# A gated attention-and-MLP kernel: Wv loaded in chunks, the first x tiles turned one by one, two small loads moved to GpSimd

## Chip, cores, metric

The kernel runs on one core of a Trainium2 chip. The metric is the device time of one launch in microseconds (us). A profile also gives the *span*, from the first to the last instruction that it counts.

## The reference, cut to what matters

```python
g = sigmoid((x * gate_w).sum(-1, keepdims=True))        # x: 2048 x 448, bf16
qkv = x @ wqkv                                           # 16 heads of 28
pq, pk = q @ w_phi, k @ w_phi                            # per head
phi_q, phi_k = [softmax(p), softmax(-p)]                 # joined
a = (phi_q @ (phi_k.T @ v)) / (phi_q @ sum(phi_k) + 1e-6) @ wo
b = gelu(x @ w1 + b1) @ w2 + b2
return g * a + (1 - g) * b
```

The kernel multiplies Wq and Wk by w_phi first (the products are called Wpq and Wpk) and carries gate_w as a 449th column of Wv, so that the gate comes out of the value matmuls.

## The kernel before

The opening, cut to the parts that the change touches. `SP`, `ACT` and `POOL` below are the engines behind `nc.sync`, `nc.scalar` and `nc.gpsimd`.

```python
for m, eng in ((0, nc.scalar), (1, nc.sync)):            # first 512 rows of x, in two halves
    eng.dma_start(x0[:, 2*m:2*m+2, :], x[m*256:(m+1)*256, :].rearrange("(t p) d -> p t d", p=P))
nc.scalar.dma_start(WvG[:, 0:3, 0:D], ...)               # Wv, 336 KB
nc.scalar.dma_start(WvG[64:P, 3, 0:D], ...)              # Wv, last 64 rows
nc.sync.dma_start(gate[0:1, :], gate_w[None, :])
nc.scalar.dma_start(wphi[:, 0:3, :], ...)
load_wT(WkT, D); load_wT(WqT, 0); load_x(1)              # transposing loads, all on SP
nc.scalar.dma_start(wphi[0:64, 3, :], wphi_rows[384:448, :])
...
dummies(7)                       # warm TensorE up
turn_x0(0, xp[0])                # 8 TensorE transposes, one copy by VectorE
turn_gate()                      # gate column -> WvG, by ScalarE
turn_x0(1, xp[1])                # 8 more, one copy by ScalarE
fill_bd()                        # VectorE, from wphi
v_pair(0, on_act=True); v_pair(1)
prep(WkT, ...); prep(WqT, ...)   # Wpk, Wpq
nc.sync.dma_start(b1c[0:NJ, :], B_b1...)
load_x(2); swap_w(WqS, Wpq); swap_x(0)    # SP: WqS and xS hold the halves of Wpq and xT swapped
load_x(3); swap_w(WkS, Wpk); swap_x(1)    # to the other 64 partitions, so that
swap_w(WvS, WvG)                          # two 64-row matmuls can run side by side
... # w1, wo loads on SP
# TensorE: k_pair, v_pair; then q pairs (need WqS, xS); k_two (WkS, xS); v_two (WvS); MLP; output
```

The softmax here doesn't subtract the row's maximum and nothing guards it: scores larger than these inputs give would overflow.

Of the kernel before, what the change touches and what calls it, by code (L numbers as in the profile page):

```python
# [13 lines left out]
D = 448  # L14
# [3 lines left out]
P = 128  # L18
# [4 lines left out]
NC4 = 4  # L23
NJ = 14
# [4 lines left out]
HP = 64  # L29

BF16 = mybir.dt.bfloat16
# [4 lines left out]
def kernel(  # L36
# [14 lines left out]
    nc = tc.nc  # L51
    x = A_x[0]
# [6 lines left out]
    ps = psx.enter_context(tc.tile_pool(name="ps", bufs=3, space=PSUM))  # L59
# [7 lines left out]
    turn = [0]  # L67

    def four(name):
        turn[0] += 1  # L70
        return wide(name) if turn[0] % 4 == 0 else pair(name)


    xT = consts.tile([P, NC4, S], BF16, name="xT")
# [11 lines left out]
    ident = consts.tile([P, P], BF16, name="ident")  # L86
# [11 lines left out]
    WvG = attn.tile([P, NC4, D + 1], BF16, name="WvG")  # L98
# [5 lines left out]
    WkT = attn.tile([P, NG, D], BF16, name="WkT")  # L104
    WqT = attn.tile([P, NG, D], BF16, name="WqT")
    wphi = attn.tile([P, NC4, DH], BF16, name="wphi")
# [4 lines left out]
    b1c = w2_sb[:, 6, 0:P]  # L111
    nc.gpsimd.memset(b1c, 0.0)
    warm = w2_sb[:, 0, 0:P]
    gate = w2_sb[:, 1, :]
# [3 lines left out]
    nc.vector.memset(WvG[0:64, 3, :], 0.0)  # L118
    nc.vector.memset(wo_sb[64:P, 3, :], 0.0)
    nc.vector.memset(Wpk[0:64, 3, :], 0.0)  # L120
    nc.vector.memset(WkT[0:1, 0, 0:1], 0.0)
    wphi_rows = A_w_phi.rearrange("h a b -> (h a) b")
    x0 = oT[:, 0, 0:4 * D].rearrange("p (t d) -> p t d", t=4)
    for m, eng in ((0, nc.scalar), (1, nc.sync)):
        eng.dma_start(x0[:, 2 * m:2 * m + 2, :],
                      x[m * 256:(m + 1) * 256, :].rearrange("(t p) d -> p t d", p=P))
    nc.scalar.dma_start(WvG[:, 0:3, 0:D],
                        A_wqkv[0:384, 2 * D:3 * D].rearrange("(c p) n -> p c n", p=P))
    nc.scalar.dma_start(WvG[64:P, 3, 0:D], A_wqkv[384:448, 2 * D:3 * D])
    nc.sync.dma_start(gate[0:1, :], gate_w[None, :])  # L130
    nc.scalar.dma_start(wphi[:, 0:3, :], wphi_rows[0:384, :].rearrange("(c p) b -> p c b", p=P))

    def load_x(b):
# [7 lines left out]
    def swap_x(h):  # L141
# [5 lines left out]
    load_wT(WkT, D)  # L147
    load_wT(WqT, 0)
    load_x(1)
    nc.scalar.dma_start(wphi[0:64, 3, :], wphi_rows[384:448, :])  # L150


    first = consts.tile([1, 1], F32, name="first")
# [1 line left out]
    nc.gpsimd.memset(ident[:], 1.0)  # L155
    nc.gpsimd.affine_select(out=ident[:], in_=ident[:], pattern=[[-1, P]],
                            compare_op=ALU.is_equal, fill=0.0, base=0, channel_multiplier=1)
    nc.gpsimd.memset(hmask[:], 1.0)
    nc.gpsimd.affine_select(out=hmask[:], in_=hmask[:], pattern=[[P, NC4], [-DH, H]],
                            compare_op=ALU.is_ge, fill=0.0, base=0, channel_multiplier=1)  # L160
# [31 lines left out]
    def copy(on_act, out, in_):  # L192
        if on_act:
            nc.scalar.copy(out=out, in_=in_)
        else:
            nc.vector.tensor_copy(out=out, in_=in_)  # L196
# [3 lines left out]
             v_ps[:, :, 0:D].rearrange("p i (x d) -> p i x d", x=NPR))  # L200
        copy(on_act, lg[:, tiles], v_ps[:, :, D])

    def v_pair(u, on_act=False, b1=False):
        v_ps = four("v_ps")
        for i in range(2):
            t = 2 * u + i
            for c in range(NC4):
                nc.tensor.matmul(v_ps[:, i, 0:D + 1], lhsT=xT[:, c, t * P:(t + 1) * P],  # L208
                                 rhs=WvG[:, c, :], start=(c == 0), stop=(c == NC4 - 1))
        if b1:  # L210
            nc.tensor.matmul(v_ps[:, 1, 480:480 + NJ], lhsT=b1c, rhs=ident[:, 0:NJ],
                             start=True, stop=True, skip_group_check=True)
        v_out(u, v_ps, slice(2 * u, 2 * u + 2), on_act)
        if b1:
            nc.vector.tensor_copy(out=b1T[:], in_=v_ps[:, 1, 480:480 + NJ])
# [114 lines left out]
                    in0=src[rows, :, i, :],  # L330
                    in1=mask[rows, None, :].to_broadcast([PW, NG, PW + 2]), op=ALU.mult)

    def turn_x0(m, tp):
        for i in range(2):
            for c in range(NC4):
                lo = c * P if c < 3 else 320
                nc.tensor.transpose(tp[:, c, i * P:(i + 1) * P], x0[:, 2 * m + i, lo:lo + P],
                                    ident[:])
        copy(m == 1, xT[:, :, m * 256:(m + 1) * 256], tp[:])

    def turn_gate():
        g_ps = four("g_ps")
        for c in range(NC4):
            lo = c * P if c < 3 else 320
            nc.tensor.matmul(g_ps[:, 0, c:c + 1], lhsT=gate[:, lo:lo + P], rhs=ident[:, 0:1],
                             start=True, stop=True)
        nc.scalar.copy(out=WvG[:, 0:3, D], in_=g_ps[:, 0, 0:3])  # L347
        nc.scalar.copy(out=WvG[HP:P, 3, D:D + 1], in_=g_ps[HP:P, 0, 3:4])

    def dummies(n):  # L350
        w_ps = four("warm_ps")
        for _ in range(n):
            nc.tensor.matmul(w_ps[:, 0, :], lhsT=warm, rhs=warm[:, None, :].to_broadcast([P, 4, P]),
                             start=True, stop=True)


    dummies(7)
    xp = [ps.tile([P, NC4, 256], BF16, name="xp", tag="pair", bufs=3) for _ in range(2)]
    turn[0] += 2
    turn_x0(0, xp[0])  # L360
    turn_gate()
    turn_x0(1, xp[1])
    fill_bd()
    v_pair(0, on_act=True)
    v_pair(1)
    prep(WkT, wk_at, (1, 0, 1))
    prep(WqT, wq_at, (1, 0, 0))
    def swap_w(W_S, W):
        nc.sync.dma_start(W_S[0:HP, :, :], W[HP:P, :, :])  # L369
        nc.sync.dma_start(W_S[HP:P, 0:3, :], W[0:HP, 0:3, :])  # L370

    nc.sync.dma_start(b1c[0:NJ, :], B_b1.rearrange("(j p) -> j p", p=P))
    load_x(2)
    swap_w(WqS, Wpq)
    swap_x(0)
# [170 lines left out]
```

## Time and profile before

| | before |
|---|---|
| time, median of three runs | 156.25 us |
| span of the profiled run | 154.9 us |
| time of the profiled run | 156.61 us |
| TensorE busy | 149.4 us |

The page has a line of the busy share of the 16 DMA engines in 40 slices of the span, and one of the bytes:

```profile
DMA  5999999999995000000000001114332123334401
...
HBM read 6.11 MB, written 1.84 MB: 51 GB/s over the span
```

The engines of the DMA are busy in the first 48 us, nearly idle for some 40 us after that and at most half busy to the end, so this is a kernel whose opening is fed by transfers and whose rest is fed by TensorE. The views that the prediction reads are the chain (what ended last, followed back from the end) and the timeline (instructions in order of time: start, duration, engine, line, operation, and in brackets the idle time before it and what ended it). SPq is the queue of transfers that SP issues.

### The profile page before, as it was taken

The numbers are of one execution on the slowest core, as the hardware profiler recorded it, in microseconds if no ns is written. First come the engines' busy times: TensorE is split into PE (matmuls) and PEld (weight loads), VectorE is DVE, ScalarE is ACT, GpSimd is POOL, SyncE is SP. The second block draws the span as 40 slices with busy tenths as digits, with TensorE's granted clock in tenths as the row PEclk, the third lists the DMA queues.
The fourth block names the chain that finished last, engine by engine and source line by source line (L and its number), as shares of the span: only waits on it lengthen the run. The fifth ranks groups of instructions, "written<-read, shape, count | busy, mean of one in ns | idle before, by whom it ended". The sixth has DMA issues, their size and how long they took to land.

```text
span 154.9 us, 3180 instructions
## 1 busy us (share of the span) xinstructions
PE 149.4 (96%) x1302; PEld 83.8 (54%) x1302; DVE 83.2 (54%) x246; ACT 77.1 (50%) x90; POOL 31.8 (21%) x34
## 2 busy tenths in 40 slices
PE   7799999999999999999999999999999999999991
PEld 2475545566666864444444455555556555555581
DVE  3444999288892050000000049999977999977100
ACT  0659759998889626777767650111311111111121
POOL 7900489919776000000000000000000000000000
PEclk9999999999999999999999999999999999999999
DMA  5999999999995000000000001114332123334401
GB/s 147 255 199 146 190 235 248 221 221 212 213 336 176 4 0 4 0 0 4 0 0 0 4 0 34 34 38 96 86 101 64 40 64 90 81 85 37 122 31 30
DMA packets 28270, 14.91 MB, mean 96 GB/s; under 512 B 20062, under 2 KB 27872, under 8 KB 28256
## 3 DMA queue, kind: packets, MB, share of 16 engines
q1 hardware_dynamic: 27024, 14.06, 42.0%
q10 hardware_dynamic: 1232, 0.66, 1.5%
q8 instruction: 10, 0.16, 0.5%
q14 instruction: 4, 0.03, 0.1%
HBM read 6.11 MB, written 1.84 MB: 51 GB/s over the span
## 4 chain that ended last, share of the span: by engine, by line
PE 79%; SPq 13%; DMA 3%; issue 1%; DVE 1%; ACT 0%; ACTq 0%
PE y L485 27%; PE hp L426 27%; PE y L491 8%; PE nm L441 4%; PE pq L307 4%; PE v_ps L291 4%; SPq L135 3%; SPq L139 3%; SPq L136 3%; DMA WvS<-WvG 3%; PE pk L299 3%; PE acc L318 2%; SPq L369 1%; SPq L370 1%; SPq L144 1%
## 5 line engine op out<-in xcount | busy, mean ns | idle before, releaser
L485 PE MATMUL y<-w_sb,gel 128*128 128x448 bf16 (+1 forms) x238 | 45.2, 341 | 0.0
L426 PE MATMUL hp<-xT,w_sb 64*128 64x512 bf16 x196 | 42.6, 376 | 0.0
L426 PE MATMUL hp<-xS,w_sb 64*128 64x512 bf16 x196 | 42.3, 376 | 0.0
L431 ACT ACTIVATE gel<-hp,b1T 128x1024 bf16<-128x1024 f32 x28 | 30.8, 1111 | 13.0 <-PE hp L426 13.0
L494 ACT ACTIVATE res<-y,ungate 128x448 bf16<-128x448 f32 (+1 forms) x17 | 10.4, 612 | 50.4 <-PE y L491 50.2
L485 PEld LDWEIGHTS <-gel 128*128 128x128 bf16 x238 | 23.1, 98 | 19.0
L426 PEld LDWEIGHTS <-w_sb 64*128 64x128 bf16 x392 | 20.5, 94 | 21.6
L268 POOL TENSOR_TENSOR phik<-phik,rec 128x1792 bf16<-128x1792 bf16 (+1 forms) x8 | 25.0, 3129 | 16.1 <-DVE rec L265 16.1
L446 DVE COPY st<-nm 128x32 f32<-128x32 f32 x32 | 4.5, 184 | 35.5 <-PE nm L441 35.5
L462 DVE TENSOR_TENSOR tmp<-nm,al 128x448 bf16<-128x448 f32 x32 | 18.4, 617 | 0.0
L263 DVE TENSOR_REDUCE sums<-phik 128x64 f32<-128x1792 bf16 x8 | 16.0, 2006 | 2.6 <-ACT phik L256 2.6
L491 PE MATMUL y<-wo_sb,oT 128*128 128x448 bf16 (+1 forms) x68 | 14.7, 341 | 0.0
L307 PE MATMUL pq<-xT,Wpq 64*128 64x512 bf16 x56 | 13.2, 376 | 0.0
L307 PE MATMUL pq<-xS,WqS 64*128 64x512 bf16 x56 | 11.5, 376 | 0.1
L196 DVE CAST vaug<-v_ps 128x896 bf16<-128x896 f32 x7 | 7.5, 1074 | 6.0 <-PE v_ps L291 3.6
L312 ACT ACTIVATE EqP<-pq 128x1024 bf16<-128x1024 f32 x8 | 8.3, 1041 | 3.7 <-PE pq L307 3.7
L313 ACT ACTIVATE EqN<-pq 128x1024 bf16<-128x1024 f32 x8 | 8.3, 1042 | 0.0
L441 PE MATMUL nm<-KVbd,EqP 128*128 128x120 bf16 x64 | 8.3, 216 | 0.0
L441 PE MATMUL nm<-KVbd,EqN 128*128 128x120 bf16 x64 | 8.3, 216 | 0.0
L255 ACT ACTIVATE phik<-pk 128x896 bf16<-128x896 f32 x8 | 7.5, 940 | 1.4 <-PE pk L277 1.4
L491 PEld LDWEIGHTS <-oT 128*128 128x128 bf16 x68 | 6.1, 98 | 3.3
L208 PE MATMUL v_ps<-WvG,xT 128*128 128x449 bf16 x32 | 6.6, 354 | 1.0 <-ACT WvG L347 1.0
(90 smaller groups left out, 145.7 us busy)
## 6 DMA issues: line engine op xcount, KB each, us to landing
w_sb<-in_B_w_dram SPq DMA_DIRECT2D x4, 784.0 KB, 14.2
out_dram<-res SPq DMA_DIRECT2D x15, 112.0 KB, 1.9
w_sb<-in_B_w_dram SPq DMA_DIRECT2D x1, 1568.0 KB, 17.3
xS<-xT SPq DMA_DIRECT2D x2, 256.0 KB, 4.0
xS<-xT SPq DMA_DIRECT2D x2, 192.0 KB, 4.3
WvG<-in_A_wqkv_dram ACTq DMA_DIRECT2D x1, 336.0 KB, 4.5
wo_sb<-in_A_wo_dram SPq DMA_DIRECT2D x1, 336.0 KB, 17.0
WqS<-Wpq SPq DMA_DIRECT2D x1, 256.0 KB, 4.6
```

Of the source, the lines that this page charges most:

```text
L263: nc.vector.reduce_sum(out=sums[:], in_=ph, axis=AX.X)
L268: eng.tensor_tensor(out=ph[:, lo:hi], in0=ph[:, lo:hi], in1=rec[:, lo:hi, :, None].to_broadcast([P, hi - lo, 2, DH]), op=ALU.mult)
L307: nc.tensor.matmul(pq[:, i, :], lhsT=w_half(Wpq, WqS, i, k)[:, g * P:(g + 1) * P], rhs=x_half(i, k, h), start=(k == 0), stop=(k == NK - 1))
L312: nc.scalar.activation(out=EqP[:, g, dst], in_=src, func=ACT.Exp)
L313: nc.scalar.activation(out=EqN[:, g, dst], in_=src, func=ACT.Exp, scale=-1.0)
L426: nc.tensor.matmul(hp[:, i, :], lhsT=w1_sb[i * HP:(i + 1) * HP, k, j * P:(j + 1) * P], rhs=x_half(i, k, h), start=(k == 0), stop=(k == NK ...
L431: nc.scalar.activation(out=gel[h][:, j, :], in_=hp[:].rearrange("p a b -> p (a b)"), func=ACT.Gelu_apprx_tanh, bias=b1T[:, j:j + 1])
L441: nc.tensor.matmul(nm[s][:, g * 2 * KW:(g + 1) * 2 * KW], lhsT=E[:, g, tok], rhs=KVbd[:, g, s, :], start=True, stop=True)
L462: nc.vector.tensor_tensor(out=tmp[:, s, :].rearrange("p (x h d) -> p x h d", x=NPR, h=2), in0=nmv[s][:, :, 0:PW].rearrange("p x (h d) -> p ...
L485: nc.tensor.matmul(y, lhsT=gel[t // 8][:, j, (t % 8) * P:(t % 8 + 1) * P], rhs=w2_sb[:, j, cols], start=(j == 0), stop=False)
L491: nc.tensor.matmul(y, lhsT=oT[:, c, tok], rhs=wo_sb[:, c, cols], start=False, stop=(c == NC4 - 1))
L494: nc.scalar.activation(out=res[:, cols], in_=y, func=ACT.Copy, scale=ungate[:, t:t + 1])
```

## The change

The intent: start the value matmuls of tile 0 as soon as its own data and the first chunk of Wv are there. Wv comes in four chunks with a wait for each. Tiles 0 and 1 are turned and copied singly, and tiles 2 and 3 between the first two value tiles. Besides, two small loads move to GpSimd's queue: the last rows of w_phi and the b1 row, the latter off SP's queue.

```diff
-    nc.vector.memset(WkT[0:1, 0, 0:1], 0.0)
-    for m, eng in ((0, nc.scalar), (1, nc.sync)):
-        eng.dma_start(x0[:, 2 * m:2 * m + 2, :], ...)
-    nc.scalar.dma_start(WvG[:, 0:3, 0:D], ...)
+    nc.scalar.dma_start(x0, x[0:512, :].rearrange("(t p) d -> p t d", p=P))
+    nc.sync.dma_start(gate[0:1, :], gate_w[None, :])
+    for c, eng in ((0, nc.sync), (1, nc.scalar), (2, nc.sync)):
+        eng.dma_start(WvG[:, c, 0:D], A_wqkv[c * P:(c + 1) * P, 2 * D:3 * D])
     nc.scalar.dma_start(WvG[64:P, 3, 0:D], A_wqkv[384:448, 2 * D:3 * D])
-    nc.sync.dma_start(gate[0:1, :], gate_w[None, :])
...
-    nc.scalar.dma_start(wphi[0:64, 3, :], wphi_rows[384:448, :])
+    nc.gpsimd.dma_start(wphi[0:64, 3, :], wphi_rows[384:448, :])
...
-        nc.scalar.copy(out=WvG[:, 0:3, D], in_=g_ps[:, 0, 0:3])
+        for c in range(3):
+            nc.scalar.copy(out=WvG[:, c, D:D + 1], in_=w_ps[:, 1, c:c + 1])
...
-    turn_x0(0, xp[0])
+    turn_x0(0, 1, False)
     turn_gate()
-    turn_x0(1, xp[1])
+    turn_x0(1, 1, False)
+    v_pair(0, on_act=True, between=lambda: turn_x0(2, 2, False))
     fill_bd()
-    v_pair(0, on_act=True)
     v_pair(1)
...
-    nc.sync.dma_start(b1c[0:NJ, :], B_b1.rearrange("(j p) -> j p", p=P))
+    nc.gpsimd.dma_start(b1c[0:NJ, :], B_b1.rearrange("(j p) -> j p", p=P))
```

More of the change, by code (lines that the diff above doesn't have):

```diff
@@ L120 @@
     nc.vector.memset(Wpk[0:64, 3, :], 0.0)
-    nc.vector.memset(WkT[0:1, 0, 0:1], 0.0)
     wphi_rows = A_w_phi.rearrange("h a b -> (h a) b")
     x0 = oT[:, 0, 0:4 * D].rearrange("p (t d) -> p t d", t=4)
-    for m, eng in ((0, nc.scalar), (1, nc.sync)):
-        eng.dma_start(x0[:, 2 * m:2 * m + 2, :],
-                      x[m * 256:(m + 1) * 256, :].rearrange("(t p) d -> p t d", p=P))
-    nc.scalar.dma_start(WvG[:, 0:3, 0:D],
-                        A_wqkv[0:384, 2 * D:3 * D].rearrange("(c p) n -> p c n", p=P))
+    nc.scalar.dma_start(x0, x[0:512, :].rearrange("(t p) d -> p t d", p=P))
+    nc.sync.dma_start(gate[0:1, :], gate_w[None, :])
+    for c, eng in ((0, nc.sync), (1, nc.scalar), (2, nc.sync)):
+        eng.dma_start(WvG[:, c, 0:D], A_wqkv[c * P:(c + 1) * P, 2 * D:3 * D])
     nc.scalar.dma_start(WvG[64:P, 3, 0:D], A_wqkv[384:448, 2 * D:3 * D])
-    nc.sync.dma_start(gate[0:1, :], gate_w[None, :])
     nc.scalar.dma_start(wphi[:, 0:3, :], wphi_rows[0:384, :].rearrange("(c p) b -> p c b", p=P))
@@ L201, in v_out, with v_pair @@
         copy(on_act, lg[:, tiles], v_ps[:, :, D])
-    def v_pair(u, on_act=False, b1=False):
+    def v_pair(u, on_act=False, b1=False, between=None):
         v_ps = four("v_ps")
@@ L206, in v_pair @@
             t = 2 * u + i
+            if i == 1 and between is not None:
+                between()
             for c in range(NC4):
@@ L331, in kv_out, with turn_x0 @@
                     in1=mask[rows, None, :].to_broadcast([PW, NG, PW + 2]), op=ALU.mult)
-    def turn_x0(m, tp):
-        for i in range(2):
+    def turn_x0(t0, n, on_act):
+        turn[0] += 1
+        if turn[0] % 4 == 0:
+            tp = ps.tile([P, NC4, n * P], BF16, name="xp", tag="acc", bufs=1)
+        else:
+            tp = ps.tile([P, NC4, n * P], BF16, name="xp", tag="pair", bufs=3)
+        for i in range(n):
             for c in range(NC4):
                 lo = c * P if c < 3 else 320
-                nc.tensor.transpose(tp[:, c, i * P:(i + 1) * P], x0[:, 2 * m + i, lo:lo + P],
+                nc.tensor.transpose(tp[:, c, i * P:(i + 1) * P], x0[:, t0 + i, lo:lo + P],
                                     ident[:])
-        copy(m == 1, xT[:, :, m * 256:(m + 1) * 256], tp[:])
-    def turn_gate():
-        g_ps = four("g_ps")
-        for c in range(NC4):
-            lo = c * P if c < 3 else 320
-            nc.tensor.matmul(g_ps[:, 0, c:c + 1], lhsT=gate[:, lo:lo + P], rhs=ident[:, 0:1],
-                             start=True, stop=True)
-        nc.scalar.copy(out=WvG[:, 0:3, D], in_=g_ps[:, 0, 0:3])
-        nc.scalar.copy(out=WvG[HP:P, 3, D:D + 1], in_=g_ps[HP:P, 0, 3:4])
+        copy(on_act, xT[:, :, t0 * P:(t0 + n) * P], tp[:])
+    w_ps = four("warm_ps")
     def dummies(n):
-        w_ps = four("warm_ps")
         for _ in range(n):
@@ L354, in dummies, with turn_gate @@
                              start=True, stop=True)
+    def turn_gate():
+        for c in range(NC4):
+            lo = c * P if c < 3 else 320
+            nc.tensor.matmul(w_ps[:, 1, c:c + 1], lhsT=gate[:, lo:lo + P], rhs=ident[:, 0:1],
+                             start=True, stop=True)
+        for c in range(3):
+            nc.scalar.copy(out=WvG[:, c, D:D + 1], in_=w_ps[:, 1, c:c + 1])
+        nc.scalar.copy(out=WvG[HP:P, 3, D:D + 1], in_=w_ps[HP:P, 1, 3:4])
     dummies(7)
-    xp = [ps.tile([P, NC4, 256], BF16, name="xp", tag="pair", bufs=3) for _ in range(2)]
-    turn[0] += 2
-    turn_x0(0, xp[0])
+    turn_x0(0, 1, False)
     turn_gate()
-    turn_x0(1, xp[1])
+    turn_x0(1, 1, False)
+    v_pair(0, on_act=True, between=lambda: turn_x0(2, 2, False))
     fill_bd()
-    v_pair(0, on_act=True)
     v_pair(1)
@@ L367, with swap_w @@
     prep(WqT, wq_at, (1, 0, 0))
-    def swap_w(W_S, W):
-        nc.sync.dma_start(W_S[0:HP, :, :], W[HP:P, :, :])
-        nc.sync.dma_start(W_S[HP:P, 0:3, :], W[0:HP, 0:3, :])
-    nc.sync.dma_start(b1c[0:NJ, :], B_b1.rearrange("(j p) -> j p", p=P))
+    def swap_w(W_S, W, eng=nc.sync):
+        eng.dma_start(W_S[0:HP, :, :], W[HP:P, :, :])
+        eng.dma_start(W_S[HP:P, 0:3, :], W[0:HP, 0:3, :])
+    nc.gpsimd.dma_start(b1c[0:NJ, :], B_b1.rearrange("(j p) -> j p", p=P))
     load_x(2)
```

## The prediction

> **What bounds the kernel now.** I read the page first (busy shares, then the chain that ended last), then that chain piece by piece, then the timeline of the first 30 us. From the page:
>
> ```profile
> span 154.9 us, 3180 instructions
> ...
> PE 149.4 (96%) x1302; PEld 83.8 (54%) x1302; DVE 83.2 (54%) x246; ACT 77.1 (50%) x90; POOL 31.8 (21%) x34
> ...
> PE 79%; SPq 13%; DMA 3%; issue 1%; DVE 1%; ACT 0%; ACTq 0%
> ```
>
> TensorE is busy for 149.4 of 154.9 us, so all that a change of the opening can win lies in the 5.5 us in which it is not. The chain, however, gives 13% of the span to the SP queue: TensorE is not the bound from the start. The chain in order of time shows where the one hands over to the other (start, duration, what):
>
> ```profile
> 2.61 0.02 DVE WkT L121
> ...
> 2.65 1.69 SPq L139
> ...
> 10.12 0.49 SPq L372
> ...
> 23.47 0.94 SPq L369
> ...
> 24.46 4.13 DMA WvS<-WvG
> ...
> 28.63 1.49 PE v_ps L291 x13
> ```
>
> From 2.65 to 24.46 us the chain is nothing but the SP queue, which issues its transfers one after the other without a gap, each in 0.5 to 2.8 us. It begins with the transpose of WkT, held back on purpose by a one-element memset (L121), and ends with the transfer of WvS, which lands at 28.59. Only then does TensorE carry the chain. The timeline shows TensorE's side of the opening (start, duration, engine, line, what, idle before it):
>
> ```profile
> 4.10 0.45 PEld L337 LDWEIGHTS <-oT 128*128 128x128 bf16 x8 [0.79 <-DMA oT<-in_A_x_dram]
> ...
> 4.57 0.24 PE L345 MATMUL g_ps<-ident,w_sb 128*128 128x1 bf16 x4
> ...
> 4.77 0.69 DVE L196 COPY xT<-xp 128x1024 bf16<-128x1024 bf16 x1 [2.15 <-PE xp L337]
> ...
> 6.10 0.17 ACT L347 CAST WvG<-g_ps 128x3 bf16<-128x3 f32 x1 [0.98 <-DMA WvG<-in_A_wqkv_dram]
> ...
> 6.29 0.16 ACT L348 CAST WvG<-g_ps 64x1 bf16<-64x1 f32 x1
> ...
> 6.32 3.23 PE L208 MATMUL v_ps<-WvG,xT 128*128 128x449 bf16 x16 [1.04 <-ACT WvG L347]
> ...
> 6.47 1.01 ACT L194 COPY xT<-xp 128x1024 bf16<-128x1024 bf16 x1
> ...
> 9.39 1.09 PE L224 MATMUL w_ps<-w_sb,WkT 128*128 128x140 bf16 x16
> ```
>
> The first x tiles land just before 4.10; the turns and the gate product are over by about 5.28; then TensorE sits idle 1.04 us until ScalarE has written the gate column into WvG, and that copy waited for the Wv transfers, 0.98 us of idle on ScalarE. From 6.32 the value tiles run, 16 matmuls in 3.2 us, until about 9.55, and TensorE then goes on without a gap until two short waits:
>
> ```profile
> 20.55 0.39 PE L307 MATMUL pq<-xT,Wpq 64*128 64x512 bf16 x1
> ...
> 21.06 0.09 PEld L307 LDWEIGHTS <-WqS 64*128 64x128 bf16 x1 [0.42 <-issue]
> ```
>
> ```profile
> 28.23 0.35 PE L291 MATMUL v_ps<-WvG,xT 64*128 64x449 bf16 x1
> ...
> 28.63 0.37 PE L291 MATMUL v_ps<-WvS,xS 64*128 64x449 bf16 x2
> ```
>
> At 20.55 the first half of a q pair starts, and its partner, which reads xS and WqS, starts at 21.06 with 0.42 us of idle before its weights. The second transfer of xS was issued at 16.46 and took 4.6 us: it landed at 21.06, so "issue" is here a DMA wait. At 28.23 the same happens with WvS: the partner should follow one step later, 0.19 us in this stretch, at 28.42, and follows at 28.63, when WvS is there: 0.2 us. After that TensorE has no wait until the last stage. So a gain of TensorE before 20.5 us alone is worth nothing: it makes these two waits longer. The end moves only as far as the landing of WvS moves, and the SP queue decides that.
>
> **What the Trainium skill says.** "DMA: Bandwidth & Descriptors", section "Issuing engines are not separate DMA queues": transfers of SP, ScalarE and GpSimd run on the same 16 engines and interleave; another issuer only saves the issue time. The trace agrees: x0 (448 KB) and Wv (392 KB), split over two queues, moved at 348 to 369 GB/s together from 2.5 to 3.5 us, and ScalarE's queue alone (4.0 to 4.5 us) reached 368. So splitting the transfers differently adds no bandwidth; saved SP issue time is what can count. Same page, "Queues, rings and completion order": each engine takes turns between the queues that have work, packet by packet. The trace of before can't test this strictly; up to 3.0 us SP's queue had moved 206 packets and ScalarE's 84, so the turns are not even at the start. "TensorE: Matmul & The Clock Gate", section "Wait — 56ns, not 53.3ns?": warm matmuls of 128 columns start every 55.6 ns. The eight turns of before started at 4.11 and the gate product after them at 4.57: 57 ns each, which agrees. Same page, Part 1: the clock falls only after about 3.4 us of idle; TensorE's granted clock is 1.00 in every half microsecond here in spite of the 1 us gap.
>
> **The change part by part.**
>
> Issue order of the first transfers. ScalarE's queue carried x0a 224, Wv 336, Wv's last rows 56 KB, sum 616; now x0 448, Wv chunk 1 112, last rows 56: 616 again. SP's carried x0b 224 KB ahead of WkT; now chunks 0 and 2, 224 KB. Bytes and first start are the same; only the order differs. x0 now has one queue and meets chunks 0 and 2 from about 2.85 us on (issued after the gate row at about 1.7, and 0.80 to 1.95 shows 1.15 us from issue to first bytes). At worst 448 + 224 KB = 688,000 bytes must have moved before x0 is there; the half-microsecond sums of before (86, 260, 445, 608, 792 thousand at 2.5 to 4.5 us) reach that at 4.2, plus about 0.35 us of completion (before, by the same sums, 3.65 to about 4.0): x0 lands at 4.6, 0.5 us later than now. Wv's last rows still come after all 860,000 bytes, so near the 5.97 of before, perhaps sooner if WkT's data start a little later: 5.7, plus or minus 0.3.
>
> TensorE. Turns of tile 0 at 4.65, four at 57 ns, 0.23 us; gate 0.24; VectorE's copy of 512 columns: the f32 casts took 1.09 us for 896 and 0.61 for 448 columns, so about 0.13 is fixed, and 0.69 for 1024 bf16 columns makes 0.41 for 512. Tile 0 can start near 5.5; its third and fourth chunk wait for the copies of gate columns 2 and 3, at 5.75 and 5.94 (0.19 apart, as 6.10 and 6.29 were). Tile 0 ends about 6.35 (before: 6.32 + 4 x 0.2 = 7.12). Then eight turns that before lay in the idle time: 8 x 57 ns = 0.46, to 6.8. Tile 1: 0.8, to 7.6. VectorE's copy of tiles 2 and 3 runs 6.9 to 7.65, so tile 2 waits 0.1 at most. Tiles 2 and 3: 1.6, to about 9.3 to 9.4. Against 9.55 that is a gain of 0.15; with the last rows at 6.0 it is a loss of 0.1. Call it p = +0.1 (-0.2 to +0.4).
>
> VectorE fills bd (1.01 us) after those copies, to about 8.7 instead of 7.3, still ahead of the product that needs it near 9.4. ScalarE loses its 1.01 us xT copy, gains two 0.17 us gate copies: not on the path.
>
> SP queue. Gone: x0b (0.46 us) and the wait for the WkT memset; new: chunks 0 and 2, about 0.5 us each. Gate at about 1.29 takes 0.35, then 2 x 0.53 with gaps: WkT at 2.75 instead of 2.65, a loss of 0.1. WqT's lane is now freed by x0's landing, perhaps 0.1 later, but it stood until 7.15 in any case. Gone at 10.05: the b1 row with its wait, 10.66 - 10.05 = 0.61 us. Sum s = 0.61 - 0.1 - (0 to 0.1) = 0.45 us earlier for all that follows: the second xS lands near 20.6, WvS near 28.15.
>
> The sum. TensorE comes to WvS at 28.42 - 0.42 - p without the xS wait, i.e. 28.63 - (0.62 + p); WvS allows 28.63 - s. The gain is the smaller of 0.62 + p = 0.72 and s = 0.45. I take 0.4, as stalls of the queue may eat part: 156.25 - 0.4 = 155.85 us.
>
> **The rivals.**
>
> First: the queue doesn't move, because its issue times are stalls of the DMA engines and not issue work. For it: WkT took 1.69 us and the equal WqT 2.77; the second WqS 1.52 against 0.60 for the like WkS, in a stretch with a 16 KB instruction fetch. Against it: between 11.5 and 12 us, and from 15 to 16, the DMA share is 0.15 to 0.45 and less, so bytes are not the bound just there. It would give 156.2 to 156.3.
>
> Second: TensorE's opening becomes worse than the shift of the queue covers: x0 at 5 us or the last rows at 6.3 make p -0.4; the gain is then 0.2, 156.05. If the turns between and the copies line up badly, p = -0.8 makes a small loss, 156.4.
>
> Third: the intent in full, tile 0 about a microsecond earlier and the end with it. Against it stand the two waits above: even p = +1 gives no more than s. For it to pay, the queue would need another 0.5 us. 155.3 at best.
>
> **Range and chances.** The terms are s (0 to 0.8) and p (-0.4 to +0.4), and the three runs of before spread over 0.35 us. Low 155.3 is the third rival with the queue at its best, high 156.5 the second with a slow run. Two per cent are 3.1 us, over half of all of TensorE's idle time; neither side is likely: 1% faster, 98% within, 1% slower.
>
> **What would show it.** x0's turns at 4.5 to 4.7; Wv's last rows landing at 5.4 to 6.0; the product after the value tiles starting at 9.2 to 9.6 (p); WqS's first issue at about 13.1 (s); the wait at the first q pair mostly gone; WvS landing at 28.0 to 28.3 and still the last thing that the chain hands to TensorE. I am wrong if WqS's issue doesn't move and the end does, if TensorE's clock falls below 1.00 in the first 10 us, or if the copy of tiles 2 and 3 or bd leaves TensorE idle for more than 0.3 us before 10 us.

## The result, and the profile after

A ratio here is the mean time of one kernel's fast runs over that of the other's fast runs of the same rounds, so it isn't quite the ratio of the medians.

| sample | changed, median (runs) | before, median (runs) | ratio, 95% interval |
|---|---|---|---|
| first | 156.60 (4) | 156.29 (4) | 1.0024 (1.0000 to 1.0049) |
| second | 156.50 (6) | 156.28 (11) | 1.0012 (0.9996 to 1.0027) |
| third | 156.73 (6) | 156.41 (11) | 1.0014 (0.9998 to 1.0031) |

By the rule of two per cent that is "same", as forecast with 98%. But 0.4 us less was forecast and the kernel is about 0.2 to 0.4 us *slower*; 156.6 lies outside the predicted range, whose upper end was 156.5. None of the three intervals excludes 1 by itself; all three lie on the same side.

The page of the changed kernel, with the lines that answer to those of before (span and instructions; busy time by engine; the DMA queue that GpSimd's transfers use, with packets, MB and share, which the page of before doesn't have; the chain by engine):

```profile
span 154.7 us, 3184 instructions
...
PE 149.8 (97%) x1302; PEld 84.8 (55%) x1302; DVE 83.9 (54%) x247; ACT 76.3 (49%) x91; POOL 33.4 (22%) x36
...
q0 software_dynamic: 64, 0.01, 0.0%
...
PE 94%; DMA 3%; SPq 0%; ACT 0%; DVE 0%; issue 0%; ACTq 0%
```

The span is *shorter* than in the profile of before, 154.7 against 154.9, while the time is longer. And in this profile the chain does not lead back over SP's queue, which had 13%. In order of time (start, duration, what):

```profile
1.69 0.38 SPq L126
...
2.12 4.13 DMA WvG<-in_A_wqkv_dram
...
6.30 0.56 PE v_ps L207 x2
6.86 0.45 PE xp L341 x8
7.30 0.77 PE v_ps L207 x4
...
8.09 1.71 PE v_ps L207 x8
9.80 1.89 PE w_ps L223 x32
...
20.86 6.19 PE pq L306 x56
...
28.37 1.48 PE v_ps L290 x14
```

In this pair of profiles the value matmuls have taken the place of SP's queue on the chain. That is not the doing of the change, as two later profiles show. The first line is the chain of the kernel before, run again (b_again below), the second that of the changed kernel, run again (a_third):

```profile
PE 94%; DMA 3%; ACTq 1%; ACT 0%; issue 0%
...
PE 84%; SPq 9%; DMA 3%; issue 1%; ACT 0%; DVE 0%; ACTq 0%
```

Which of the two the chain follows changes from run to run of the same kernel.

In the chain of the changed kernel above, the wait in front is the last Wv chunk of SP's queue (issued at 2.12, landed at 6.25); the product after the value tiles starts at 9.8 in this view. The first matmul that reads WvS runs at 28.37 (28.63 before). From the timeline (columns as above):

```profile
2.58 2.34 SPq L136 DMA_TRANSPOSE WkT<-in_A_wqkv_dram  x1
...
4.08 0.34 PEld L341 LDWEIGHTS <-oT 128*128 128x128 bf16 x4 [0.76 <-DMA oT<-in_A_x_dram]
...
4.97 2.58 SPq L136 DMA_TRANSPOSE WqT<-in_A_wqkv_dram  x1
...
5.22 0.56 PE L207 MATMUL v_ps<-WvG,xT 128*128 128x449 bf16 x2
...
6.30 0.56 PE L207 MATMUL v_ps<-WvG,xT 128*128 128x449 bf16 x2 [0.53 <-DMA WvG<-in_A_wqkv_dram]
...
10.44 1.73 SPq L132 DMA_TRANSPOSE xT<-in_A_x_dram  x1
...
13.65 0.56 SPq L371 DMA_DIRECT2D WqS<-Wpq  x1
```

and the same SP issues in the timeline of before:

```profile
4.38 2.77 SPq L139 DMA_TRANSPOSE WqT<-in_A_wqkv_dram  x1
...
10.66 1.45 SPq L135 DMA_TRANSPOSE xT<-in_A_x_dram  x1
...
13.59 0.57 SPq L369 DMA_DIRECT2D WqS<-Wpq  x1
```

Tile 0's first matmul does start a microsecond earlier (5.22 against 6.32), as intended. After two chunks it waits for the next. WkT's issue takes 2.34 us (before: 1.69), WqT starts at 4.97 instead of 4.38, and WqS at 13.65 instead of 13.59, although the b1 row, 0.61 us of issue and wait, has gone from between.

One pair of profiles says 0.2 us shorter, the clock says longer. So two questions were open: what lies outside the span, and whether the 0.2 us within it are real.

### The profile page after: what moved, and what is told of

Read it like the earlier page. It is cut to its first block, busy times and chain, and to the rows that moved or that the text cites. A ratio compares the mean times of both kernels' runs of the same rounds, so it can differ in the third digit from the quotient of the medians.

```text
span 154.7 us, 3184 instructions
## 1 busy us (share of the span) xinstructions
PE 149.8 (97%) x1302; PEld 84.8 (55%) x1302; DVE 83.9 (54%) x247; ACT 76.3 (49%) x91; POOL 33.4 (22%) x36
## 3 DMA queue, kind: packets, MB, share of 16 engines
HBM read 6.11 MB, written 1.84 MB: 51 GB/s over the span
## 4 chain that ended last, share of the span: by engine, by line
PE 94%; DMA 3%; SPq 0%; ACT 0%; DVE 0%; issue 0%; ACTq 0%
PE y L487 27%; PE hp L428 27%; PE pq L306 8%; PE y L493 8%; PE nm L443 4%; PE v_ps L207 4%; PE pk L276 4%; PE v_ps L290 4%; PE pk L298 3%; DMA WvG<-in_A_wqkv_dram 3%; PE acc L317 2%; PE w_ps L223 1%; ACT res L496 0%; PE xp L341 0%; SPq L126 0%
## 5 line engine op out<-in xcount | busy, mean ns | idle before, releaser
L306 PE MATMUL pq<-xS,WqS 64*128 64x512 bf16 x56 | 12.1, 376 | 0.0
L207 PE MATMUL v_ps<-WvG,xT 128*128 128x449 bf16 x32 | 7.1, 355 | 0.5 <-DMA WvG<-in_A_wqkv_dram 0.5
```

The costliest lines, as they stand in the source:

```text
L207: nc.tensor.matmul(v_ps[:, i, 0:D + 1], lhsT=xT[:, c, t * P:(t + 1) * P], rhs=WvG[:, c, :], start=(c == 0), stop=(c == NC4 - 1))
L306: nc.tensor.matmul(pq[:, i, :], lhsT=w_half(Wpq, WqS, i, k)[:, g * P:(g + 1) * P], rhs=x_half(i, k, h), start=(k == 0), stop=(k == NK - 1))
```

## Experiments

Eighteen runs. Each kernel of a call ran on the same chip beside 11 runs of the kernel before. The table gives means over all timed runs of each; "span, diff." is the mean span less that of before in the same call; "on GpSimd" is the number of transfers that GpSimd issues.

| run | time ratio (95%) | span | span, diff. | time minus span | on GpSimd |
|---|---|---|---|---|---|
| before | 1 | 154.50 to 154.80 | 0 | 1.70 to 1.73 | 0 |
| a_again (changed) | 1.0012 (0.9996 to 1.0027) | 154.53 | -0.04 | 1.95 | 2 |
| a_third (changed) | 1.0014 (0.9998 to 1.0031) | 154.77 | -0.03 | 1.96 | 2 |
| a_nopool | 1.0027 (1.0011 to 1.0043) | 154.93 | +0.36 | 1.73 | 0 |
| a_act | 0.9990 (0.9973 to 1.0007) | 154.42 | -0.15 | 1.73 | 0 |
| b_pool | 1.0013 (0.9998 to 1.0028) | 154.55 | -0.02 | 1.95 | 2 |
| b_again (before) | 0.9995 (0.9975 to 1.0014) | 154.60 | -0.05 | 1.72 | 0 |
| b_act | 0.9989 (0.9970 to 1.0007) | 154.47 | -0.18 | 1.72 | 0 |
| a_one | 1.0001 (0.9979 to 1.0022) | 154.68 | +0.03 | 1.70 | 1 |
| best1 | 1.0111 (1.0088 to 1.0134) | 156.37 | +1.72 | 1.73 | 0 |
| a_xs | 0.9999 (0.9980 to 1.0018) | 154.57 | -0.23 | 1.95 | 2 |
| b_xs | 0.9982 (0.9968 to 0.9996) | 154.14 | -0.66 | 2.11 | 2 |
| a_w | 1.0016 (0.9995 to 1.0037) | 155.07 | +0.27 | 1.70 | 1 |
| b_two | 0.9991 (0.9974 to 1.0007) | 154.45 | -0.35 | 1.97 | 2 |
| b_three | 1.0007 (0.9989 to 1.0026) | 154.50 | -0.30 | 2.12 | 3 |
| best3 | 1.0100 (1.0081 to 1.0119) | 156.44 | +1.64 | 1.71 | 1 |
| b_one | 0.9995 (0.9982 to 1.0008) | 154.42 | -0.08 | 1.70 | 1 |
| b_xs1 | 1.0022 (0.9987 to 1.0056) | 154.85 | +0.35 | 1.70 | 1 |
| b_xs_again | 1.0009 (0.9997 to 1.0021) | 154.26 | -0.24 | 2.10 | 2 |

Within one kernel single spans differ by up to 1.0 us (1.7 in b_xs1), so a difference of means of 6 and 11 runs is good to about 0.2 us (estimated from a standard deviation of 0.2 us between runs: twice the root of 0.04/6 + 0.04/11). Time minus span is far steadier: within a kernel it varies by no more than 0.12 us, and part of that is rounding, as spans are recorded to 0.1 us.

The second table has points of the profiles, in us: when the product after the value tiles starts on TensorE, the first q pair and its half that reads xS, the issue of WqS and WvS on SP, and the first matmul that reads WvS.

| profile | product | q | q, xS half | WqS issue | WvS issue | WvS read |
|---|---|---|---|---|---|---|
| before | 9.39 | 20.55 | 21.06 | 13.59 | 23.47 | 28.63 |
| b_again | 9.58 | 20.74 | 20.96 | 13.68 | 23.37 | 28.52 |
| changed | 9.64 | 20.79 | 20.85 | 13.65 | 23.18 | 28.36 |
| a_again | 9.46 | 20.61 | 20.73 | 13.69 | 23.06 | 28.21 |
| a_third | 9.30 | 20.46 | 20.99 | 13.51 | 23.35 | 28.48 |
| a_act | 9.11 | 20.27 | 20.83 | 13.42 | 23.14 | 28.19 |
| b_act | 9.63 | 20.79 | 20.79 | 13.52 | 23.12 | 28.21 |
| b_xs | 9.31 | 20.46 | 20.47 | 14.31 | 22.37 | 27.85 |
| a_xs | 9.28 | 20.47 | 20.47 | 14.02 | 22.10 | 27.85 |

In every profile, these and the others, the last matmul ends 123.06 to 123.08 us after the first read of WvS. Everything behind that point is rigid: the change can act only before it, and outside the span.

### a_again: the changed kernel again

> The changed kernel unaltered, run again for a larger sample beside the kernel before on one chip. The two profiles said: every point of TensorE's work from 28.4 us on lies 0.25 to 0.27 us earlier than before, yet the time was 0.3 us longer, because time minus span was 2.0 us in all its four runs and 1.7 in the one profiled run of before. Theory A (the two transfers issued by GpSimd cost time outside the span): again time minus span near 2.0 here and 1.7 for before, span 0.1 to 0.3 shorter, time 0.0 to 0.4 longer. Rival N (the difference of time minus span was chance): both have the same time minus span, and the time is 0.2 to 0.3 shorter than before.

Measured: time minus span 1.95 in all six runs within 0.03, before 1.73 in all eleven within 0.06. The span is 0.04 shorter, not 0.2. The numbers are those of theory A, and the rival is out: the difference isn't chance.

A third sample:

> The changed kernel once more beside the kernel before. Time minus span 1.95 against 1.72 (theory A). What the change wins within the span is open: the profiles say 0.25 us, the spans of the timed runs 0.0 to 0.1. Theory C (the profiles of before happened to be slow samples): span 0.0 to 0.15 below before, time 0.1 to 0.25 above. Prediction's view: span 0.3 to 0.45 below before and time 0.1 to 0.2 below or equal.

Measured: span -0.03 against before, time minus span 1.96, ratio 1.0014. These are the numbers of theory C; the 0.2 to 0.3 of gain in the span, which the pair of profiles suggested, did not come.

### a_nopool: the new opening without GpSimd transfers

```diff
-    nc.gpsimd.dma_start(wphi[0:64, 3, :], ...)
+    nc.scalar.dma_start(wphi[0:64, 3, :], ...)      # just after the first activation
-    nc.gpsimd.dma_start(b1c[0:NJ, :], ...)
+    nc.sync.dma_start(b1c[0:NJ, :], ...)            # the old place
```

> The changed kernel with its two GpSimd transfers taken back: the last rows of w_phi on ScalarE's queue (just after the first activation), the b1 row on SP's at its old place; the opening otherwise as changed. Theory A: time minus span 1.7, and the queue gives back the issue time of the b1 row, so the span is 0.0 to 0.3 longer than the changed kernel's; time 156.1 to 156.4, within 0.15 of before. Rival O (it is the new opening, its order of transfers or its greater number of instructions, that costs time outside the span): time minus span stays at 2.0 and the time is 156.6 to 156.9.

Measured: time minus span 1.73, as theory A says, but the time is 0.27% *above* before, by an interval that excludes 1: the span is 0.36 us above before and 0.40 above the changed kernel's, more than the 0.0 to 0.3 expected for giving the row back. So the new opening by itself costs within the span. That had been in neither theory. The load of w_phi's rows comes later here than in either kernel; a_act, which has it at the same place, shows that this isn't the cause.

### a_act: both small loads on ScalarE's queue

```diff
-    nc.gpsimd.dma_start(wphi[0:64, 3, :], ...)
+    nc.scalar.dma_start(wphi[0:64, 3, :], ...)      # just after the first activation
+    nc.scalar.dma_start(b1c[0:NJ, :], ...)          # after turn_gate()
-    nc.gpsimd.dma_start(b1c[0:NJ, :], ...)
```

> The changed kernel with the same two transfers moved to ScalarE's queue, the b1 row after the gate copies, so that neither GpSimd nor SP issues it. Theory A: the shorter span of the changed kernel (0.25 below before) with a time minus span of 1.7: time 155.9 to 156.1, 0.3 below the changed kernel run beside it... and 0.2 below before. Rival O: time as the changed kernel's, 156.5 to 156.7.

Measured: median 156.13, time minus span 1.73, 0.34 us (0.2%) below the changed kernel in the means of the same call (156.15 and 156.49). What was expected against the changed kernel came; against before the gain, 0.15, isn't clear of noise.

### b_pool: only the two GpSimd transfers, in the kernel before

```diff
-    nc.scalar.dma_start(wphi[0:64, 3, :], ...)
+    nc.gpsimd.dma_start(wphi[0:64, 3, :], ...)      # after the identity is built
-    nc.sync.dma_start(b1c[0:NJ, :], ...)
+    nc.gpsimd.dma_start(b1c[0:NJ, :], ...)
```

> The kernel before with nothing but the two transfers moved to GpSimd, at the places that the change gives them. Theory A: time minus span 2.0 instead of 1.7, while SP's queue, relieved of the b1 row, lets WvS land 0.3 to 0.5 earlier and the span shrink by 0.2 to 0.4: time within 0.15 of before. Rival O: time minus span 1.7 and the time 0.2 to 0.4 below before.

Measured: time minus span 1.95 with the old opening. Together with a_nopool this separates the two: the cost outside the span follows the GpSimd transfers and not the opening (rival O is out). The span hardly moved (-0.02), less than expected.

### b_again: the kernel before again

> The kernel before, unaltered, as a control, for a second profile. Its eleven runs of the last call had a mean span of 154.57 us; the one profile that the prediction was read from has 154.9, so it was a slow sample. In all six profiles the last matmul ends 123.07 or 123.08 us after the first matmul that reads WvS. Theory C (the waits for xS and WvS that the prediction counted on are shorter in a usual run of before, so there was less to win): this profile's first read of WvS near 28.3, not 28.6, and the sum of the two waits 0.2 to 0.4 instead of 0.6. Rival: it shows 28.5 to 28.7 again with the full waits, and the run-to-run spread comes from after that point, where the 123.07 would then differ.

Measured: a part of each. Its profile reads WvS at 28.52, which is the rival's number; the waits of about 0.2 (q) and 0.2 (WvS), 0.4 together, are theory C's. The 123.07 us are the same, against the rival's second clause. The profiled run, 154.8, was again one of the longer of its six (mean 154.60). So the two profiles of before that could be read are both slower than its average run by 0.2 to 0.3 us, and this is most of the 0.2 us by which the changed kernel's profiles look shorter. Theory C holds in direction.

### b_act: only the b1 row off SP's queue

```diff
-    nc.sync.dma_start(b1c[0:NJ, :], ...)
+    nc.scalar.dma_start(b1c[0:NJ, :], ...)          # after v_pair(1)
```

> The kernel before with only the b1 row moved from SP's to ScalarE's queue, behind the copies of the first value pair: the relief of SP's queue alone, without GpSimd. Theory C: TensorE's own work bounds a usual run of before almost as early as the queue does, so the span shrinks by 0.0 to 0.15 us and no more, and time minus span stays 1.73: time 156.1 to 156.3. Prediction's view (the queue is the bound and 0.45 us can be had from it): WvS read 0.3 to 0.45 earlier, time 155.8 to 156.0.

Measured: span -0.18, near theory C's limit of 0.15 and well short of 0.45; the time ratio is not clear of 1. The profile alone would have said otherwise: WvS is read at 28.21, 0.31 and 0.42 earlier than in the two profiles of before, as in the prediction's view; but those two are slow samples. The row was worth 0.61 us in the prediction. The SP issues show where it stays. In the two profiles of before the x transpose that follows the row took 1.45 and 1.46 us. In all eleven profiles with no b1 row on SP and nothing else moved there it took 1.60 to 1.89, though it is the same transfer. On average it gives back about 0.25 of the 0.61. The rest does move the queue: in the five kernels with the old opening and only small loads moved (b_act, b_pool, b_two, b_three, b_one) WqS is issued at 13.23 on average, 0.41 earlier than in the two profiles of before.

### a_one and a_w: one GpSimd transfer, late or early

```diff
 # a_one: b1 stays on GpSimd              # a_w: w_phi's rows stay on GpSimd
-    nc.gpsimd.dma_start(wphi[...])       -    nc.gpsimd.dma_start(b1c[...])
+    nc.scalar.dma_start(wphi[...])       +    nc.scalar.dma_start(b1c[...])
```

> The changed kernel with only one of its two GpSimd transfers left (the b1 row; the last rows of w_phi on ScalarE's queue). If the cost outside the span is paid once for having any transfer on GpSimd, time minus span is 1.95 as with two; if it is paid per transfer, 1.84. The span as the changed kernel's, 154.4 to 154.7.

> Which of the two GpSimd transfers costs the 0.22 us outside the span? With the b1 row alone on GpSimd time minus span was 1.70, as without any. Here the last rows of w_phi alone are on GpSimd, at 1.5 us, the b1 row on ScalarE's queue. If the cost belongs to this early transfer: 1.95. If it needs two transfers on GpSimd: 1.72.

Measured: 1.70 with either one. Neither of the numbers offered for a_one (1.95 or 1.84) came. A single transfer on GpSimd costs nothing outside the span, whichever it is. a_w's mean span has one long run (155.7) in it, and without that it is still +0.07; nothing is built on it.

### b_two and b_three: the b1 row by GpSimd twice and three times

```diff
-    nc.sync.dma_start(b1c[0:NJ, :], ...)
+    nc.gpsimd.dma_start(b1c[0:NJ, :], ...)
+    nc.gpsimd.dma_start(b1c[NJ:2 * NJ, :], ...)     # rows that meet zeros of the identity
+    nc.gpsimd.dma_start(b1c[2 * NJ:3 * NJ, :], ...) # b_three only
```

> The kernel before with the b1 row loaded by GpSimd, late, twice (the second copy goes to rows that are multiplied by zeros of the identity, so the result stays right). If the cost needs two transfers on GpSimd: time minus span 1.95. If it belongs to the early transfer of w_phi's rows: 1.72. The span 154.3 to 154.6.

> The kernel before with the b1 row loaded three times by GpSimd, late. Two GpSimd transfers cost 0.23 to 0.27 us outside the span whatever they were, one cost nothing. If the cost is one step from the second transfer on: time minus span 1.95 to 1.98. If each transfer after the first adds as much: 2.2. Span 154.3 to 154.7.

Measured: 1.97 with two, 2.12 with three. So the second transfer adds about 0.25 us and the third 0.15, here. Of the two forecasts for b_three neither is met: it grows, but by less than the first step. As b_two's transfers are both late, an early one isn't needed.

### a_xs and b_xs: a real relief of SP's queue, for both openings

```diff
 # on top of a_act and of b_act
-    swap_x(0)
+    swap_x(0, nc.gpsimd)
```

> The changed kernel without its two GpSimd transfers (both on ScalarE's queue) and with the first pair of xS transfers moved from SP's queue to GpSimd's, which is idle from 9 to 17 us. In eight of nine profiles so far the first read of WvS comes 5.05 to 5.18 us after the issue of WvS, so the queue sets it. Here SP has 1.3 us less to issue before WkS, and xS can land near 16 instead of 20.8. Theory Q (the queue sets the end of the opening in both kernels and hides whatever TensorE wins before 20 us): the first q pair runs without a wait, the first read of WvS is at pq + 7.4, about 27.7 instead of 28.2, the span 153.9 to 154.1, time 155.6 to 155.8, if these late GpSimd transfers cost nothing outside the span, 155.8 to 156.0 if they cost 0.22. Rival: the transfers on GpSimd's queue are slow or disturb the transposes, and the span stays at 154.4.

> The same relief (b1 row on ScalarE's queue, first xS pair on GpSimd's) given to the kernel before. With the queue out of the way, the difference to the sibling run shows what the new opening is worth on TensorE's own path: in nine profiles the first q pair starts at 20.49 us on average in kernels with the new opening and at 20.75 with the old, so 0.2 to 0.3 us: span 154.1 to 154.4. If the queue still binds, both have the same span.

The chain of b_xs in order of time, at the place where the waits were:

```profile
20.53 6.15 PE pq L307 x56
...
28.00 1.33 PE v_ps L291 x14
```

Measured: with two large transfers off SP's queue both profiles run from the first q pair to the read of WvS without a wait and read WvS at 27.85, 0.7 to 0.8 us earlier than before. b_xs has the shortest mean span of all, 0.66 below before. In the profiles theory Q holds: the queue was in the way. The timed runs show less of it: a_xs is 0.23 below before where a_act, without this relief, was 0.15 below, and b_xs run again (below) 0.24. The second half of the expectation is wrong. The new opening is worth nothing on TensorE's own path: both q pairs start at 20.46 and 20.47, and a_xs has in fact the longer mean span of the two by 0.43 (two of its six runs, 154.7 and 155.2, make half of that). And 0.25 to 0.4 us of the gain goes outside the span.

### best1: the gate row issued after the Wv chunks

```diff
 # on top of a_act
-    nc.sync.dma_start(gate[0:1, :], ...)
     for c, eng in ((0, nc.sync), (1, nc.scalar), (2, nc.sync)):
         eng.dma_start(WvG[:, c, 0:D], ...)
+    nc.sync.dma_start(gate[0:1, :], ...)
```

> The changed kernel without GpSimd transfers (w_phi's last rows and b1 on ScalarE's queue) and with SP's first three issues reordered: Wv chunks 0 and 2 go first, from 0.80 us on, and the gate row, which must wait for its memset at 1.24, after them, so SP no longer stands until 1.27. If SP's queue still sets the end there (in the profile without GpSimd the second xS transfer, issued 16.09, held TensorE until 20.83), all of SP's issues come 0.4 us earlier, the second xS lands near 20.4 and the first read of WvS is at 27.8 to 28.0 instead of 28.2: time 155.7 to 155.9. Rival: the queue stands before the first WqS transfer, which needs Wpq from TensorE and VectorE, so nothing after it moves, and the time is 156.0 to 156.2.

Measured: 1.1% slower, far outside both theories. First three lines of the timeline; then a table of stretches, whose columns are the stretch and its length, the busy time of PE, PEld, DVE, ACT and POOL with their counts in brackets, the granted clock, the DMA share and GB/s:

```profile
5.12 0.40 PE L341 MATMUL xp<-ident,oT 128*128 128x128 bf16 x4 [0.90 <-DMA oT<-in_A_x_dram]
...
6.17 0.24 PE L355 MATMUL warm_ps<-ident,w_sb 128*128 128x1 bf16 x4 [0.65 <-DMA w_sb<-in_gate_w_dram]
...
8.16 3.84 PE L207 MATMUL v_ps<-WvG,xT 128*128 128x449 bf16 x12
```

```profile
6.00:7.00 1.00, 0.82 (x10) 0.59 (x11) 0.30 (x1) 0.45 (x4) 0.99 (x2) 1.00 1.32 263
...
8.00:9.00 1.00, 1.00 (x7) 0.55 (x5) 0.60 (x1) 0.00 (x0) 0.00 (x0) 0.50 1.28 290
...
11.00:12.00 1.00, 1.00 (x8) 0.56 (x7) 0.00 (x0) 0.00 (x0) 0.00 (x0) 1.00 0.88 162
```

SP's first issues now begin at 0.80, and x0 shares the DMA engines from its first byte: it lands at 5.1 instead of 4.05. TensorE is idle for 0.90 us, then for 0.65 until the gate row is there. After that its clock is taken down: granted 1.00 until 7 us, 0.50 from 8 to 10, and 12 value matmuls take 3.84 us, where 16 took 3.23 before. That the idle times are the reason is read from the order of events in one profile; no run tests it. The half microsecond of SP's wait for a memset, which looked like waste, had kept x0's way free.

### best3 and b_xs1: attempts to have the relief with one GpSimd transfer

```diff
 # best3, on top of before                   # b_xs1, on top of b_act
+    swap_x(0, (0,), nc.scalar)  # first half
-    swap_x(0)                                -    swap_x(0)      # first half on SP as before,
+    swap_x(0, (1,), nc.gpsimd)               +    swap_x(0, nc.gpsimd)  # helper: second half only
-    swap_w(WvS, WvG)
+    swap_w(WvS, WvG, nc.scalar) # before v_pair(3)
```

> The kernel before with its old opening and b1 on SP's queue, and three transfers taken off SP's queue by using idle time of others: the first xS half on ScalarE's queue at about 9.1 us, the second on GpSimd's (only one transfer there, so nothing outside the span), the WvS pair on ScalarE's queue at about 21 us. Theory Q and the step from one to two GpSimd transfers together: the first q pair runs without a wait, first read of WvS near 27.9, span 154.1 to 154.3, time minus span 1.72, time 155.8 to 156.0, 0.4 below before. If ScalarE's issues delay its copies, TensorE waits for PSUM and the span stays above 154.4.

> The kernel before with the b1 row on ScalarE's queue and only the second of the first two xS transfers on GpSimd's, a single transfer there. Theory Q: SP's queue is relieved by 1.2 us from there on, the first q pair runs without its wait, first read of WvS 27.9 to 28.1; span 154.2 to 154.4, time minus span 1.72, time 0.4 to 0.6 below before, the best of all. If the data on GpSimd's queue slow SP's transposes, as in the last attempt, no gain.

From the chain of best3, and then from that of b_xs1:

```profile
18.47 2.46 SPq L136
...
23.13 5.96 DMA xS<-xT
```

```profile
16.37 2.65 SPq L135
19.07 2.56 SPq L136
```

Measured: best3 is 1.0% slower. Its x transposes on SP take up to 2.46 us (1.62 before) with copies of other queues in flight, and the second xS transfer of the later pair takes 5.96 us to land (4.0 to 4.6 before), beside WvS on ScalarE's queue. b_xs1 falls into two groups: four runs of 155.86 to 156.36 and two of 157.48 and 157.62, the profiled one among them. In that profile the transposes behind the GpSimd transfer take 2.65 and 2.56 us (1.88 and 1.62 before). So the clause named in advance, transposes slowed by data of another queue, fits both. It is not shown to be the cause: in b_pool, where no large copy had moved, one x transpose took 2.38 us too.

### b_one and b_xs_again

```diff
 # b_one, on top of before
-    nc.sync.dma_start(b1c[0:NJ, :], ...)
+    nc.gpsimd.dma_start(b1c[0:NJ, :], ...)
```

> The kernel before with only the b1 row moved from SP's to GpSimd's queue: the one part of the change that relieves SP's queue, with a single GpSimd transfer. If the gain within the span comes from this relief (spans so far 0.02, 0.18, 0.35 and 0.30 below before in four kernels with the old opening and the b1 row off SP's queue) and one GpSimd transfer costs nothing outside: span 0.1 to 0.35 below before, time minus span 1.72, time 0.1 to 0.35 below before, and below the changed kernel by 0.3 to 0.5.

> The kernel that was fastest so far (b1 row on ScalarE's queue, both first xS transfers on GpSimd's), again, because its time minus span of 2.11 didn't fit the 1.95 of the other three kernels with two GpSimd transfers. Chance: 1.95 now. A property of this kernel: 2.11 again. Span 0.5 to 0.7 below before, time 0.2 to 0.4 below.

Measured: b_one is as before within noise (span -0.08, time minus span 1.70), 156.12 in the mean. Against the changed kernel it can be compared only across calls: its ratio to before is 0.9995, the changed kernel's 1.0012 to 1.0024. b_xs_again has 2.10 outside the span again, so that was not chance: with two GpSimd transfers four kernels have 1.95 to 1.98 and this one 2.10. The number of transfers isn't the whole rule. Nor is it the packets on queue q0, which every profile with a GpSimd transfer has and no other: 64 packets in one transfer left 1.70 and 1.71 (b_xs1, best3), 64 in two gave 1.95 to 1.98, and 144 in two gave 1.95 in a_xs and 2.10 to 2.11 in b_xs. And its gain of 0.18% isn't confirmed: 1.0009 now. No version tried beats the kernel before for certain.

## Why the prediction was wrong, step by step

**The sum (wrong, a term was missing).** The prediction took the time to move with the landing of WvS. The time has a part outside the span that the change makes longer: 1.72 to 1.95 us, by 0.23. a_again, a_third and b_pool show it with the two GpSimd transfers, a_nopool and a_act show it gone without them. b_two shows it with two others. No step of the prediction had this term; it took GpSimd as a free issuer. Where it lies in the launch (before the first counted instruction or after the last) no run shows. The Trainium skill's page "Runtime: NRT & Kernel Launch", section "The ~15µs preamble/postamble breakdown", lists a reset of the DMA rings after the kernel and says that the total depends on the "DMA setup"; that would fit, but it is only argued.

**The SP term s = 0.45 (mis-sized).** Its removal of the b1 row, 0.61 us, was right as an issue time; but about 0.25 of it comes back in the transpose behind, which is longer without the row. Its loss in front was set at 0.1 to 0.2. It measured about 0.3: the second x transpose starts at 9.01 to 9.14 in the three profiles of the changed kernel (mean 9.07) and at 8.74 and 8.82 before (mean 8.78), which is 0.29; over all profiles with either opening, best1 and best3 left out, the means are 9.04 and 8.68. WkT's issue with two Wv chunks ahead of it took 2.34 to 2.61 us, not 1.69. So 0.61 - 0.25 - 0.3 leaves about 0.05. That is what WqS's issue shows: 13.62 in the mean of three profiles against 13.64 of two. The prediction had named 13.1 there; of its sign of being wrong, "if WqS's issue doesn't move and the end does", the first half came true. WvS was issued 0.22 earlier on average (23.20 and 23.42), in profiles of which those of before are slow samples. The spans of timed runs, 0.04 and 0.03 shorter, good to about 0.15 together (estimated from the 0.2 for one), say that s was close to nothing. The first rival, a queue that stands for its transfers rather than for issue work, was nearer than the main line: both losses are issues that last longer. It isn't the whole truth, as taking off the row alone does move WqS's issue, by 0.41.

**TensorE's term p = +0.1 (right in size).** The product after the value tiles starts at 9.47 in the mean of three profiles, before at 9.49; p is 0.02, inside the range given (0.08 over all profiles with either opening, best1 and best3 left out: 9.32 and 9.40). The intended early start is real (5.2 to 5.4 instead of 6.3) and is given back: tile 0 waits for its later chunks, and the eight turns that had lain in idle time now lie between the value tiles. Details of the path were off: x0 landed at 4.05 and not at 4.6, because SP's chunks, issued at 1.69, had moved at most 2 packets by 3.5 us while ScalarE's queue had moved 521. Wv's last rows landed at about 5.95 (issued at 1.84, landed 4.1 later), inside the range given; but the second chunk on SP's queue, whose landing the prediction had not worked out, came at 6.25, and tile 0 waited for it.

**The smaller of the two (right in form).** Gain = the smaller of 0.62 + p and s. Taken with the one pair of profiles that the prediction started from, p = -0.25 and s = 0.29 or less at WvS, and the WvS read moved by 0.27. Against the same profile of before, a_again has s = 0.41 and moved by 0.42, a_third 0.12 and 0.15. And b_xs, with the queue out of the way, shows the waits gone and the span 0.66 shorter in its call (0.24 in b_xs_again).

**The baseline (a choice that went wrong).** The two waits of 0.62 us came from one profile, of a run of 156.61 us, the longest of the four then known. A usual run of before is 0.1 to 0.4 us shorter than that profile's 154.9, so part of that 0.62 was never there to be won. The chain with 13% on SP's queue was this profile's too: b_again's has none.

**The parts against each other.** New opening alone: +0.36 us in the span (a_nopool). b1 row off SP alone, old opening: -0.02, -0.18, -0.35, -0.30 and -0.08 in five kernels. Together: -0.04 and -0.03 (the parts, with the mean of the five, make +0.17; the 0.2 between is as large as the error of such a sum). Then +0.23 outside. The two that were measured together, -0.03 and +0.23, are the +0.2 us seen.

The remaining chances: the class "same" at 98% was right; the third rival (the intent in full) has a_xs and b_xs against it, in one profile each; the second rival gave 156.05 to 156.4 for the wrong reason, a bad p.

Left open: why two GpSimd transfers cost time outside the span and one doesn't, why b_xs costs 0.15 more than its siblings, and why a transpose takes longer without the b1 row ahead of it.

## What to carry to other kernels

Look at time and span separately for every version: a gain in the trace can be paid back where the trace doesn't look, here by a second transfer on an otherwise unused GpSimd queue. An issue time on a queue full of transposes is not a saving until the issue behind it has been seen to move; read the start of the next fixed point (here WqS), not the length of the piece removed. Take the baseline's waits, and its chain, from more than one profile when the whole stake is half a microsecond.

## What the Trainium skill lacked or had wrong

- "DMA: Bandwidth & Descriptors", section "Issuing engines are not separate DMA queues": says that another issuer saves sequencer time. It lacks that transfers on GpSimd can lengthen the launch outside the trace: 1.70 to 1.73 us with none or one, 1.95 to 1.98 with two in four kernels, two large ones in a_xs among them, 2.10 to 2.12 with three small ones (b_three) and with two large ones in b_xs.
- The same page, "Queues, rings and completion order": engines take turns between queues packet by packet. It lacks what this makes of two queues at the start: in the changed kernel at most 2 packets of SP's queue had gone by 3.5 us against 521 of ScalarE's, with SP's issues 0.9 us later; in the kernel before it was 194 against 84 between 2 and 3 us. With SP's chunks issued at 0.80 instead of 1.69, x0 landed at 5.1 instead of 4.05 us. This doesn't refute the turns: the trace's packets are about 900 bytes here (0.46 MB in 521), and they need not be the page's.
- The same page, "DMA Transpose (X-bar)": no word on what copies do to transposes beside them. WkT's issue took 1.62 to 1.73 us behind the half of x0, 2.34 to 2.77 behind two Wv chunks; the fifth and sixth x transposes 1.59 to 1.92 in two profiles of before, 2.38 in b_pool, and up to 2.65 with large copies of other queues (b_xs1).
- "TensorE: Matmul & The Clock Gate", Part 1: the clock is said to fall after an idle window of about 3.4 us; a later section adds that short idle times between groups of matmuls can do it too, without a size. In best1 the granted clock fell to 0.50 though no idle time between matmuls after the first was longer than 0.90 us; but TensorE had been busy only 0.63 us of the 2.00 between 4 and 6 us. Before, a single idle time of 1.04 us, with 0.96 us busy of the 2.00 between 5 and 7 us, left it at 1.00. That several short idle times close together were enough in best1 is read from one profile.
